# q, k and v laid out token by token, and third blocks of two experts gathered one expert earlier

## The chip, the cores and the metric

The kernel runs on one core of one Trainium2 chip. The metric is the device time of one execution in microseconds (us). Before the change the median of three runs is 735.86 us (735.72 to 737.33).

The engines are named as in the profile: PE is TensorE, with PEld its weight loads; DVE is VectorE, ACT is ScalarE, POOL is GpSimd, SP is SyncE. A q behind the name (SPq) is the engine's own sequencer, which issues transfers. All transfers share 16 DMA engines.

## What is computed

Three layers, one after the other, in float32. First causal attention by blocks of 64 tokens: 4 batches, 8 heads, 576 tokens, 64 numbers a head. Then a dense layer (512 to 2048, ELU, back to 512) on all 2304 tokens. Then a layer of 8 experts of which each token uses at most one:

```
scores = scale * np.matmul(q, k.transpose(0, 1, 3, 2))      # masked by blocks of 64, softmax
x = attn_out.transpose(0, 2, 1, 3).reshape(B * S, H * D)
h = x @ w_in
x = np.where(h > 0, h, np.exp(np.minimum(h, 0)) - 1) @ w_out
...
do_compute = x @ w_skip > 0
e_idx = argmax(xc @ w_gate)                                  # xc: the tokens with do_compute
y[e_idx == e] = gate_w * (relu(xc @ w1[e]) @ w2[e])
out[do_compute] = xc + y
```

q, k and v come as (batch, head, token, number). With the given inputs the eight experts get 176, 2, 5, 91, 283, 192, 453 and 14 tokens.

## The kernel before

**The planner.** Most of the work isn't issued as it is written. A recorder collects the instructions of a stage with their reads and writes, gives each a cost, and puts them in an order for each engine; then it issues them. That is why most rows of the profile name line 320, where recorded instructions are issued. The cost of a transfer goes by its bytes and doubles where the innermost run of its pattern is under 512 B. The order on an engine is fixed once issued; only semaphores decide when an instruction starts.

**The front.** `load_raw` (line 668) loads a tile of 128 tokens (64 for the last of a batch) of q, k or v: 128 rows by 8 heads by 64 numbers, 256 KB, into one of five `raw` tiles. In DRAM the eight heads of a token lie apart, so the pattern walks 256 B runs. `prep_k`, `prep_q` and `prep_v` split the tile on ACT and DVE into two float16 parts; k and q are then transposed, by TensorE for the first two tiles of batch 0, by a transposing transfer for the others. `vflat` (line 621) loads all of a batch's v flat, for a scale. In between, `raw_load` brings the weights of the dense layer (tiles `rw`, 512 KB each), which `conv` turns from 64-bit into 32-bit floats on DVE (tiles `twi`, `two`). All these loads go out on SP's queue in the order that the planner gave. The attention units of all batches and the dense layer run interleaved until about 560 us.

**The experts.** From there the code has branches on the number of tokens. The order is expert 0, 6, 4, 5 (`ORDER`), then 1, 2, 3 and 7 together (`LAST`). A first block of 128 tokens each of experts 0 and 6 is done ahead. A block is up to 128 tokens (the first of most experts is 64): a gather by POOL of 128 rows of `pay_d` into one of three staging tiles `gp`, a transposing transfer on SP into a place x (half of one of four tiles `X2`; `mxt` and `mxwo` in the rows), two layers of matmuls, and a scatter by POOL that adds to the output. Block (e, j) is block j of expert e. `place_of` (line 1719) names its place: all blocks j >= 2 of the four use the fourth tile, half j % 2.

Who gathers a block beside which other block stands in three tables. `GATHERS` (line 1734) are those beside a first block (`first_tokens`, line 1775). `PREP` (line 1736) lists by expert, and by part between bars, what is done beside its first, second and third block: l and m load half of an expert's weights, s takes their norm, c scales it, p splits them, and g gathers; "g1-0" is block (1, 0). `more_tokens` (line 1815) opens a branch for block j: it runs the block with its part of `PREP`, and where the branch isn't taken the else side does the rest of `PREP` alone. A loop inside it (line 1826) also gathers further blocks of the same expert. `the_rest` (line 1851) handles blocks past the fourth (the third for expert 0).

Of the kernel before, what the change touches and what calls it, by code (L numbers as in the profile page):

```python
# [356 lines left out]
@with_exitstack  # L357
def tile_kernel(ctx, tc, q, k, v, w_in, w_out, w_skip, w_gate, w1, w2, out):
    nc = tc.nc
    B, H, S, D = q.shape  # L360
    NT, DM = out.shape
    DFF = w_in.shape[1]
    E = w_gate.shape[1]
# [18 lines left out]
    rc = Recorder(nc)  # L382
# [237 lines left out]

    def vflat(b):
        t = ap.tile([128, H * S * D // 128], F32, tag="kt1", bufs=1, name="vflat")
        rc.sync.dma_start(out=t, in_=v[b].rearrange("h s d -> (h s d)").rearrange("(p x) -> p x", p=128))
        st["vf", b] = t

    def vmax(b):
# [38 lines left out]
    def trows(n):  # L665
        return 128 if n < 4 else 64

    def load_raw(nm, b, n):
        src = {"q": q, "k": k, "v": v}[nm]
        r = trows(n)  # L670
        t = ap.tile([128, H, D], F32, tag="raw", bufs=5, name="raw")
        rc.sync.dma_start(out=t[0:r], in_=src[b, :, n * 128:n * 128 + r, :].rearrange("h p d -> p h d"))
        RAW[nm, b, n] = t

    def early(b, n):
# [554 lines left out]
    def L(nm, b, n):  # L1230
        return lambda: load_raw(nm, b, n)
# [4 lines left out]
    for b in range(B):  # L1236
        g0, g1 = ubase[b, 0], ubase[b, 1]
# [83 lines left out]
    VF = [4, 5, 6, 6, 7, 8, 9]  # L1321
    rc.base = -300
    load_raw("k", 0, 0)
    load_raw("q", 0, 0)
    load_to(2)
    load_raw("k", 0, 1)
    load_raw("q", 0, 1)
    vflat(0)
    setup_consts()
    rc.gpsimd.tensor_copy(out=ident16, in_=ident)  # L1330
# [22 lines left out]
    for b in range(1, 4):  # L1353
        on_q(0, VF[b - 1], lambda b=b: vflat(b))
        on_q(0, VF[b + 2], lambda b=b: vmax(b))
# [213 lines left out]
    for i in range(2):  # L1569
        t = wp.tile([128, 2, PW], F32, tag=f"wo{i + 4}", bufs=1, name=f"gp{i}")  # L1570
# [24 lines left out]
    X2 = [AH["x"], mo.tile([128, 8, 256], F16, tag="xt", bufs=3, name="mxt1")]  # L1595
# [12 lines left out]
    def gather(ix, xT):  # L1608
        gp = GP[ng[0] % 3]
        ng[0] += 1  # L1610
        rc.gpsimd.indirect_dma_start(out=gp, out_offset=None, in_=pay_d[:, :],
                                     in_offset=bass.IndirectOffsetOnAxis(ap=ix, axis=0), bounds_check=NT - 1, oob_is_err=False)
        rc.sync.dma_start_transpose(out=xT, in_=gp.bitcast(F16))
# [94 lines left out]
    def block(*args):  # L1708
        for _ in block_in_parts(*args):
            pass  # L1710
# [4 lines left out]
    ORDER = [0, 6, 4, 5]  # L1715
    LAST = [1, 2, 3, 7]
    XP = {0: 1, 6: 2, 4: 0, 5: 1}

    def place_of(e, j):
        if e in LAST:  # L1720
            i = LAST.index(e)
            h = (X2[2 - i // 2 * 2], i % 2) if j == 0 else (X2[1], 1) if j == 1 else (X2[3], j % 2)
        else:
            h = X2[XP[e] if j < 2 else 3], j % 2
        return h[0][:, :, 128 * h[1]:128 * h[1] + 128]

    def gather_to(e, j):
        gather(gix[:, e, C0[e] + j:C0[e] + j + 1], place_of(e, j))

    def pre_gather(e):  # L1730
        for j in range(2):
            gather_to(e, j)

    GATHERS = {0: [], 6: [(6, 2), (4, 0), (4, 1)], 4: [(4, 2)], 5: [(5, 2)]}

    PREP = {int(e): [x.split() for x in h.split("|")] for e, h in (y.split(":") for y in (
        "6:l1-1 m2-0 c5-0 p5-0 s1-0|g5-0 g5-1 c5-1 p5-1|g1-0 g2-0 c1-0 s1-1,4:l2-1 m7-0 p1-0 c1-1|p1-1 s2-0|g3-0 g7-0 c2-0 s2-1,"
        "5:l7-1 l3-0 p2-0 c2-1|p2-1,8:a3-1 s7-0 s7-1 c7-0 p7-0 c7-1 p7-1").split(","))}

    def aside_of(e, part):  # L1740
        return PREP.get(e, [])[part:part + 1]
# [8 lines left out]
    def split_beside(e, part):  # L1750
        for h in sum(aside_of(e, part), []):
            if h[0] == "m":
                load_half(int(h[1]), int(h[3]), 5.0)
            if h[0] == "g":
                gather_to(int(h[1]), int(h[3]))
            if h[0] in "almg":
                continue
            for kind, f in prep_steps(int(h[1]), int(h[3]), 13.0 if e == 8 else 3.0):
                if kind[1] == {"s": "t", "c": "c", "p": "p"}[h[0]]:
                    rc.atom()  # L1760
                    rc.shift = -150000 if kind == "scale" else 0
                    f()
                    if h[0] == "s":
                        rc.ready[len(rc.steps) - 1] = 4.0
                    rc.shift = 0

    def tokens(e, j, xT, fs, par=None, block=block):

        c = C0[e] + j
        if j == 0 and e in SMALL:  # L1770
            return block(e, xT[:, :, 64:128], hix[:, e, c:c + 1], half[:, e, c, 1:2], j if par is None else par, 64)
        else:
            return block(e, xT, six[:, e, c:c + 1], fs[:, c:c + 1], j if par is None else par)

    def first_tokens(e, fs):

        rc.begin()
        rc.late = rc.left
        rc.strict = e in (4, 5)
        rc.urgent = True  # L1780
        load_beside(e, 0)
        tokens(e, 0, place_of(e, 0), fs)
        rc.urgent = False
        for g in GATHERS[e]:
            gather_to(*g)
        split_beside(e, 0)
        rc.issue()
# [23 lines left out]
    def hint(e, j, n):  # L1811

        tc.mark_branch_hint_location(f"n{e}_{j}", n > 128 * j, engines=[mybir.EngineType.PE])

    def more_tokens(e, j, fs):

        aside = j and aside_of(e, j)
        now = rc.left
        keep = list(FREE), dict(RAW2), dict(WHL)
        with tc.If(cnt[e] > 128 * j, preferred_fallthrough_block=True, label=f"n{e}_{j}") as cmp:  # L1820
            if j < BLOCKS[e]:
                hint(e, j + 1, cnt[e])
                rc.begin()
                rc.late = rc.left if j else {}
                rc.urgent = True
                for x in {6: (3,), 4: (3,), 5: (), 0: (1, 2)}.get(e, (1, 2, 3)) if j == 1 else (3,) if (e, j) == (5, 2) else ():
                    gather_to(e, x)
                tokens(e, j, place_of(e, j), fs)
                rc.urgent = False
                if aside:  # L1830
                    split_beside(e, j)
                rc.issue()
                now = rc.left
                more_tokens(e, j + 1, fs)

            else:
                the_rest(e, fs)
        if aside:
            with cmp.Else():
                FREE[:] = keep[0]  # L1840
                for x, y in ((RAW2, keep[1]), (WHL, keep[2])):
                    x.clear()
                    x.update(y)
                rc.begin()
                for part in range(j, len(PREP[e])):
                    split_beside(e, part)
                rc.issue()
        if j == 1:
            rc.left = now

    def the_rest(e, fs):

        trips = nc.values_load(ni[0:1, 8 + e:9 + e], min_val=BLOCKS[e], max_val=NS)
        sel = sm.tile([128, 3, NS], F32, tag="rw", bufs=1, name="sel")
        cj = sm.tile([128, 4], F32, tag="mx", bufs=4, name="cj")
        ci_ = sm.tile([128, 2], I32, tag="si", bufs=1, name="cji")
        nc.vector.memset(cj[:, 0:1], float(C0[e] + BLOCKS[e] - 1))
        nc.gpsimd.iota(sel[:, 0], pattern=[[1, NS]], base=0, channel_multiplier=0, allow_small_or_imprecise_dtypes=True)
        with tc.For_i(BLOCKS[e], trips):
            nc.vector.tensor_scalar(out=cj[:, 0:1], in0=cj[:, 0:1], scalar1=1.0, scalar2=None, op0=ALU.add)  # L1860
            nc.vector.tensor_scalar(out=sel[:, 1], in0=sel[:, 0], scalar1=cj[:, 0:1], scalar2=None, op0=ALU.is_equal)
            for x, src in ((1, gix[:, e, :]), (2, six[:, e, :]), (3, fs)):
                nc.vector.tensor_tensor(out=sel[:, 2], in0=sel[:, 1], in1=src, op=ALU.mult)
                nc.vector.tensor_reduce(out=cj[:, x:x + 1], in_=sel[:, 2], axis=AX.X, op=ALU.add)
            nc.vector.tensor_copy(ci_, cj[:, 1:3])
            gather(ci_[:, 0:1], X2[3][:, :, 0:128])
            block(e, X2[3][:, :, 0:128], ci_[:, 1:2], cj[:, 3:4], 0)

    gather_to(0, 0)
    pre_gather(6)  # L1870
# [109 lines left out]
```

## Time and profile before

| | us |
|---|---|
| median of 3 runs | 735.86 |
| the profiled execution | 739.06 |
| its span, first to last instruction | 736.9 |
| PE busy | 674.6 |
| DVE busy | 577.1 |
| ACT busy | 513.8 |
| POOL busy | 82.0 |

A row of a timeline gives start, duration, engine, line, operation, the tile written and the tiles read, the count, and in brackets how long the engine was idle before and what released it. The transfer view counts packets in a stretch, and the share of the 16 DMA engines' time that each queue took (it can pass 100%, as transfers overlap within an engine).

### The profile page before, as it was taken

To read this page: it belongs to the slowest core of one execution; us is meant where nothing else is said; L and a number is where in the kernel's file an instruction comes from. 1 tells how busy PE (TensorE), PEld (TensorE's weight loads), DVE (VectorE), ACT (ScalarE), POOL (GpSimd) and SP (SyncE) were. 2 spreads that over 40 slices of the span, in tenths; PEclk is the share of its full clock that TensorE was granted. 3 is DMA by queue.
4 is the path that set the end of the run, shared out by engine and by line. 5 is a ranking of instruction groups with operands and counts; after the bars stand their busy time and mean duration, and the time that the engine had idled before them with its cause. 6 is when DMAs were issued, how large, how long until landed. Compare 5 with 4: busy or idle time off the path is not lost. (4 is left out here: it accounts for less than half of the span.)

```text
span 736.9 us, 17737 instructions
## 1 busy us (share of the span) xinstructions
PE 674.6 (92%) x6665; PEld 463.8 (63%) x6665; DVE 577.1 (78%) x1664; ACT 513.8 (70%) x1090; POOL 82.0 (11%) x121
## 2 busy tenths in 40 slices
PE   4678988999999999989999999999999999999794
PEld 3456633775466666647656667667575667687583
DVE  5887999987999999878969946999687645666462
ACT  5966746999986887678668736865465638696482
POOL 2000000001001000100100100100114135333112
PEclk9669999999999999999999999999999999999897
DMA  9999999888696999899439259626265688999631
GB/s 264 229 257 304 282 277 270 177 159 163 128 199 136 187 182 189 148 198 186 90 79 181 46 93 293 256 91 197 71 215 121 191 176 247 179 284 219 176 117 16
DMA packets 262123, 134.00 MB, mean 182 GB/s; under 512 B 233467, under 2 KB 234501, under 8 KB 261504
## 3 DMA queue, kind: packets, MB, share of 16 engines
q1 hardware_dynamic: 256816, 123.33, 72.8%
q0 software_dynamic: 4112, 7.23, 4.6%
q10 hardware_dynamic: 1088, 2.10, 0.9%
q8 instruction: 57, 0.93, 0.5%
q14 instruction: 50, 0.41, 0.2%
HBM read 74.12 MB, written 12.75 MB: 118 GB/s over the span
## 5 line engine op out<-in xcount | busy, mean ns | idle before, releaser
L320 PE MATMUL h<-xt,win 128*128 128x256 f16 x1344 | 158.5, 273 | 1.6 <-DVE n L320 1.0
L320 PE MATMUL y<-wout,g 128*128 128x512 f16 x672 | 155.7, 379 | 0.0
L320 PEld LDWEIGHTS <-win 128*128 128x128 f16 x1344 | 129.0, 98 | 25.0 <-issue 2.8
L320 PEld LDWEIGHTS <-g 128*128 128x128 f16 x672 | 64.1, 98 | 66.6
L320 ACT ACTIVATE e<-s,mx 128x512 f32<-128x512 f32 (+4 forms) x160 | 82.3, 517 | 26.0 <-DVE mx L320 10.4
L320 ACT ACTIVATE ehl<-e,su 128x512 f16<-128x512 f32 (+4 forms) x160 | 80.5, 550 | 22.7 <-DVE su L320 10.3
L320 DVE SCALAR_TENSOR_TENSOR ehl<-e,su,ehl 128x512 f16<-128x512 f32 (+4 forms) x160 | 81.9, 537 | 11.3 <-ACT ehl L320 11.1
L320 PE MATMUL s<-kt,qt 128*128 128x384 f16 (+5 forms) x384 | 69.2, 306 | 10.7 <-ACT e L320 7.2
L320 DVE TENSOR_REDUCE mx<-s 128x1 f32<-128x512 f32 (+4 forms) x160 | 74.4, 474 | 5.1 <-PE s L320 4.8
L320 PE MATMUL h<-xt,twi 128*128 128x256 f32 x256 | 60.4, 388 | 2.4 <-DVE g L320 2.0
L320 PE MATMUL xps<-et,vt 128*64 128x128 f16 (+1 forms) x1440 | 49.6, 217 | 13.8 <-DVE xt L320 3.0
L320 PE MATMUL y<-two,g 128*128 128x512 f32 x128 | 59.5, 603 | 1.5 <-DVE two L320 1.5
L320 PEld LDWEIGHTS <-vt 128*64 128x64 f16 x1440 | 39.8, 113 | 32.2 <-issue 23.1
L320 ACT ACTIVATE el<-h,col 128x512 f32<-128x512 f32 x56 | 38.2, 682 | 24.7 <-PE h L320 23.8
L320 PEld LDWEIGHTS h<-xt,twi 128*128 128x128 f32 x256 | 48.2, 193 | 9.6 <-DVE g L320 2.5
L320 ACT ACTIVATE g<-el,col 128x512 f16<-128x512 f32 x56 | 40.1, 718 | 18.6 <-DVE el L320 17.2
L320 PEld LDWEIGHTS <-p 128*128 128x128 f16 x984 | 46.6, 98 | 9.9 <-PEq L1820 4.1
L320 PEld LDWEIGHTS <-qt 128*128 128x128 f16 (+1 forms) x384 | 28.2, 103 | 28.6 <-issue 11.2
L320 DVE SCALAR_TENSOR_TENSOR g<-el,col,g 128x512 f16<-128x512 f32 x56 | 41.7, 744 | 3.7 <-ACT g L320 3.6
L1521 DVE SCALAR_TENSOR_TENSOR p<-p,n,p 128x1024 f16<-128x1024 f32 x32 | 40.7, 1281 | 3.5 <-ACT p L1520 3.4
L320 DVE SCALAR_TENSOR_TENSOR el<-h,col,el 128x512 f32<-128x512 f32 x56 | 41.7, 744 | 1.3
L320 DVE TENSOR_TENSOR hh<-r,hh 128x256 f16<-128x256 f32 x36 | 15.0, 423 | 34.3 <-ACT hh L1666 32.7
(234 smaller groups left out, 1145.1 us busy)
## 6 DMA issues: line engine op xcount, KB each, us to landing
p<-in_moe_w_dram SPq DMA_DIRECT2D x45, 512.0 KB
rw<-in_moe_w_in_dram SPq DMA_DIRECT2D x16, 512.0 KB
rw<-in_moe_w_out_dram SPq DMA_DIRECT2D x16, 512.0 KB
pb<-in_moe_w_dram SPq DMA_DIRECT2D x10, 512.0 KB
vflat<-in_v_dram SPq DMA_DIRECT2D x4, 1152.0 KB
out_dram<-pay SPq DMA_DIRECT2D x18, 256.0 KB
pay_d<-pay SPq DMA_DIRECT2D x18, 256.0 KB
raw<-in_k_dram SPq DMA_DIRECT2D x16, 256.0 KB
```

The lines of the kernel that those rows point to most:

```text
L320: rec.call(e, time, lambda: getattr(self.real, op)(*args, **kw), reads, writes, dma)
L1521: rc.call("dve", 1.2, lambda: nc.vector.scalar_tensor_tensor(out=half(1), in0=raw.t, scalar=sc, in1=half(0), op0=ALU.mult, op1=ALU.subtrac ...
```

## The change

q, k and v are handed over as (batch, token, head, number), rearranged on the host. A row of a `raw` tile is then one stretch of 2 KB in DRAM; the pattern is still written with three levels, so that the planner's cost for it is what it was.

In the experts, the third blocks of 4 and 5 are gathered one expert earlier: (4, 2) beside (6, 2), and (5, 2) beside (4, 2). They leave `GATHERS` and the loop in `more_tokens` and enter `PREP`. (4, 2) and (4, 3) get the second half of the fourth tile; the third and fourth blocks of 6 and 5 use the first. A fourth block (j = 3) of 6, 4 or 5 is gathered only inside its own branch, where before it was gathered beside the second block, for 6 and 4.

```
-    B, H, S, D = q.shape
+    B, S, H, D = q.shape
...
-        rc.sync.dma_start(out=t, in_=v[b].rearrange("h s d -> (h s d)").rearrange("(p x) -> p x", p=128))
+        rc.sync.dma_start(out=t, in_=v[b].rearrange("s h d -> (s h d)").rearrange("(p x) -> p x", p=128))
...
-        rc.sync.dma_start(out=t[0:r], in_=src[b, :, n * 128:n * 128 + r, :].rearrange("h p d -> p h d"))
+        rc.sync.dma_start(out=t[0:r], in_=src[b, n * 128:n * 128 + r])
...
-            h = X2[XP[e] if j < 2 else 3], j % 2
+            h = (X2[XP[e]], j % 2) if j < 2 else (X2[3], e == 4)
...
-    GATHERS = {0: [], 6: [(6, 2), (4, 0), (4, 1)], 4: [(4, 2)], 5: [(5, 2)]}
+    GATHERS = {0: [], 6: [(6, 2), (4, 0), (4, 1)], 4: [], 5: []}
...
-        "6:l1-1 m2-0 c5-0 p5-0 s1-0|g5-0 g5-1 c5-1 p5-1|g1-0 g2-0 c1-0 s1-1,4:l2-1 m7-0 p1-0 c1-1|p1-1 s2-0|g3-0 g7-0 c2-0 s2-1,"
+        "6:l1-1 m2-0 c5-0 p5-0 s1-0|g5-0 g5-1 c5-1 p5-1|g1-0 g2-0 g4-2 c1-0 s1-1,4:l2-1 m7-0 p1-0 c1-1|p1-1 s2-0|g3-0 g7-0 g5-2 c2-0 s2-1,"
...
-                for x in {6: (3,), 4: (3,), 5: (), 0: (1, 2)}.get(e, (1, 2, 3)) if j == 1 else (3,) if (e, j) == (5, 2) else ():
+                for x in {0: (1, 2)}.get(e, () if e in ORDER else (1, 2, 3)) if j == 1 else (3,) if j == 3 and e in ORDER else ():
...
-            gather(ci_[:, 0:1], X2[3][:, :, 0:128])
-            block(e, X2[3][:, :, 0:128], ci_[:, 1:2], cj[:, 3:4], 0)
+            gather(ci_[:, 0:1], place_of(e, 2))
+            block(e, place_of(e, 2), ci_[:, 1:2], cj[:, 3:4], 0)
...
-        a = _np.ascontiguousarray(inputs[name])
+        a = inputs[name]
+        a = _np.ascontiguousarray(a.transpose(0, 2, 1, 3) if name in "qkv" else a)
```

## Rows read from the trace of the kernel before

**Rows 1.** The page: PE's busy time, and its granted clock in 40 slices.

```profile
PE 674.6 (92%) x6665; PEld 463.8 (63%) x6665; DVE 577.1 (78%) x1664; ACT 513.8 (70%) x1090; POOL 82.0 (11%) x121
...
PEclk9669999999999999999999999999999999999897
```

**Rows 2.** Busy time by stretch: length, each engine, granted clock, DMA share, GB/s.

```profile
20.00:30.00 10.00, 7.27 (x62) 4.99 (x62) 9.11 (x34) 8.97 (x26) 0.00 (x0) 0.53 1.00 289
...
90.00:100.00 10.00, 8.90 (x43) 4.02 (x42) 10.00 (x23) 4.43 (x9) 0.00 (x0) 1.00 1.13 267
...
140.00:150.00 10.00, 10.00 (x126) 8.30 (x125) 9.07 (x31) 10.00 (x28) 0.95 (x1) 1.00 0.90 169
```

**Rows 3.** PE's waits, 140 to 300 us: total, times, longest.

```profile
PE xps L320 <- DMA et<-ehl: 2.1, 3, 1.5
```

**Rows 4.** Timeline of PE in the experts' stage.

```profile
641.48 3.06 PE L320 MATMUL hp<-mxt,p 128*128 128x64 f16 x96 [0.95 <-ACTq L1820]
...
658.25 4.18 PE L320 MATMUL hp<-mxwo,p 128*128 128x128 f16 x72
...
669.87 0.44 PE L320 MATMUL hp<-mxt,p 128*128 128x64 f16 x9 [0.89 <-ACTq L1820]
...
689.27 0.19 PE L320 MATMUL hp<-mxwo,pd 128*128 128x64 f16 x1
693.47 0.29 PE L320 MATMUL hp<-mxwo,pd 128*128 128x64 f16 x2 [4.00 <-issue]
693.58 3.75 PE L320 MATMUL hp<-x,p 128*128 128x128 f32 x16
...
706.51 2.05 PE L320 MATMUL hp<-x,p 128*128 128x128 f32 x16
```

**Rows 5.** Packets moved at 13.6 to 14.6, 16.2 to 17.6 and 6.8 to 9.6 us.

```profile
DMA packets 1103, 0.28 MB, mean 278 GB/s; under 512 B 1103, under 2 KB 1103, under 8 KB 1103
...
DMA packets 282, 0.54 MB, mean 389 GB/s; under 512 B 16, under 2 KB 16, under 8 KB 282
...
DMA packets 2111, 0.71 MB, mean 254 GB/s; under 512 B 2010, under 2 KB 2010, under 8 KB 2111
```

**Rows 6.** The same view, 582.5 to 584 us, while the lists load: packets, MB, share.

```profile
q1 hardware_dynamic: 977, 0.17, 62.8%
```

**Rows 7.** Timelines of ACT and DVE in the front: uses of loaded tiles.

```profile
4.14 0.63 ACT L320 ACTIVATE k<-raw 128x512 f16<-128x512 f32 x1 [2.05 <-DMA raw<-in_k_dram]
...
9.34 0.43 DVE L320 TENSOR_SCALAR twi<-rw 128x512 int32<-128x512 int32 x1 [1.05 <-DMA rw<-in_moe_w_in_dram]
...
10.39 0.63 ACT L320 ACTIVATE k<-raw 128x512 f16<-128x512 f32 x1 [0.67 <-DVE twi L320]
...
49.09 0.63 ACT L320 ACTIVATE qq<-raw 128x512 f16<-128x512 f32 x1 [2.69 <-DMA raw<-in_q_dram]
...
61.09 0.43 DVE L320 TENSOR_SCALAR twi<-rw 128x512 int32<-128x512 int32 x1 [3.02 <-DMA rw<-in_moe_w_in_dram]
...
105.54 0.43 DVE L320 TENSOR_SCALAR two<-rw 128x512 int32<-128x512 int32 x1 [1.04 <-DMA rw<-in_moe_w_out_dram]
```

**Rows 8.** Timeline of SP's queue: issue of the first and second k.

```profile
0.81 0.46 SPq L320 DMA_DIRECT2D raw<-in_k_dram  x1
...
3.42 0.47 SPq L320 DMA_DIRECT2D raw<-in_k_dram  x1
```

**Rows 9.** SP's queue in the experts' stage: weight loads, two transposes, that of (5, 2).

```profile
656.37 2.00 SPq L1466 DMA_DIRECT2D p<-in_moe_w_dram  x4
...
668.97 3.11 SPq L320 DMA_TRANSPOSE mxt<-gp  x2
...
684.54 2.74 SPq L320 DMA_TRANSPOSE mxwo<-gp  x1
```

**Rows 10.** Busy time by stretch around and after the pause; columns as in rows 2.

```profile
693.50:697.00 3.50, 3.50 (x18) 3.50 (x19) 0.43 (x1) 0.80 (x2) 0.00 (x0) 0.50 0.03 7
```

**Rows 11.** Packets by queue, 690.6 to 691 us: packets, MB, share.

```profile
q8 instruction: 1, 0.02, 22.3%
```

## The prediction

> **What bounds the kernel now.** I read the page first, then busy time by stretch, then the timelines of single engines and the transfer view where an engine waited. TensorE is busy 92% of the span, and its granted clock falls to 6 tenths in the second and third of the 40 slices, 18 to 55 us [rows 1]. So the bound changes with the stage. In 20 to 30 us VectorE and ScalarE carry the load (9.11 and 8.97 of 10 us) and TensorE is 7.27 of 10; in 90 to 100 us VectorE is full; from 140 us TensorE is full [rows 2]. The 16 transfer engines are at or above a share of 1.0 in two of these three stretches. Before 140 us a transfer that lands earlier can therefore still move the end, because everything after it is an order fixed in advance with little idle time; after 140 us it can do so only where TensorE itself waits for a transfer, and between 140 and 300 us the largest such wait sums to 2.1 us [rows 3]. In the expert stage TensorE goes from block to block with gaps of about 1 us at the borders (0.89 us before expert 5) and with one pause of 4.00 us in the middle of a block, which the profile puts down to nothing it can see [rows 4].
>
> **The layout: what one load costs.** A full q, k or v tile is 256 KB. Before, each row gathers eight runs of 256 B, one for each head, so 1024 packets. In a stretch that holds nothing else, such packets move at 278 GB/s; in one with hardly any short packets the rate is 389 GB/s [rows 5]. That makes 0.92 to 0.94 us against 0.67 us: 0.25 us a load. Where two of these loads overlap the tail of weight loads, 2010 short packets took 2.8 us, 1.4 us for each tile [rows 5]; against 0.67 that would be 0.7 us a load, the upper bound. There are 48 full and 12 half tiles, together 54 full ones: 13.5 us of transfer time taken off, most of it where nobody waits.
>
> Will the runs really become 2 KB? The pattern still names three levels on both sides (row, head, 64 numbers), but now the last two are contiguous in memory and in the tile. The nearest row is the load of the lists, written with four levels of which the last two are contiguous in DRAM: if every pair of numbers (8 bytes) were a packet, its 152 KB would be 19,456 packets, but the stretch that holds nearly all of it has 977 on that queue, 0.17 MB [rows 6], about 174 B each. So contiguous levels are joined. I take 2 KB. The planner still reads 256 B from the pattern, so its costs, and with them the order of the front, stay.
>
> **The layout: the sum.** Step 1, the start: ScalarE waits 2.05 us for the first k, VectorE follows and TensorE begins [rows 7]. Between the issue at 0.81 [rows 8] and this use at 4.14 us lie 3.3 us, of which the data's own 0.92 us falls to 0.67. Lower bound 0.25 us; upper bound 1.0, if the slow ramp before full rate also comes from the number of packets. I take 0.6, between them, as no row separates the two. Step 2, the second k (issued at 3.42, used at 10.39 us [rows 7, 8]): ahead of it in the queue are k, q and two weight loads, so it gains 0.25 twice plus its own 0.25 to 0.7. But VectorE must first convert the weights for which it waits 1.05 us at 9.34 [rows 7]; they gain only the 0.5 us of k and q. I take 0.6 beyond step 1, near those weights' 0.5, since VectorE's own order sets this stretch; bounds 0 and 0.9. From there to 40 us ScalarE and VectorE are full and keep the shift. Step 3, the later waits: q at 49.09 us (2.69 us of waiting) gains its own 0.25 to 0.7, taken 0.4; the wait of 3.02 us at 61.09 is for weights issued before the next k, so 0; weights at 105.54 us (1.04 us) [rows 7] have one k directly ahead, 0.25; smaller ones 0.1. Together 0.75, bounds 0 and 2. Step 4, after 140 us: 0.2, bounds 0 and 0.5. Sum 0.6 + 0.6 + 0.75 + 0.2 = 2.15 us, bounds 0.25 and 4.4. A loss is possible only if earlier transfers upset a later order; I give it 0.5 us. The flat load of v for the scale stays contiguous and costs 0.
>
> **The gathers.** The experts' blocks in this run are three of expert 6, three of 4, two of 5; no fourth block runs and expert 5 has no third. So before, the gathers and transposes for (6, 3), (4, 3) and (5, 2) are made for nothing; after, the first two are gone and (5, 2) stays. Needed and moved is only (4, 2), from beside (4, 0) to beside (6, 2). Its block begins at 658.25 us right behind the one before [rows 4], so the move earns 0 there: that wait doesn't exist. The cover in the new place is all of (4, 0) and (4, 1), the 16.8 us from 641.48 to 658.25 [rows 4], so it costs 0 too; without that cover a gather and its transpose would stand open in front of the block. The queues: on SyncE the weight loads at 656.37 stand behind the transpose of (4, 2) today [rows 9]; without it they can follow the loads before them at once, and nothing before the last stage reads them. In the new place the transpose of (4, 2) stands before the weight loads of the first block of 4 and may push them by its 1.3 us; their readers come two blocks later: 0. On GpSimd the gather waits for one of three staging tiles, and the scatter of (6, 2) is queued behind it; that scatter holds an output tile that is wanted two blocks later: 0. Beside (4, 2) a third transpose now stands ahead of the loads in the first block of 5. Today's two took 3.11 us [rows 9], so it delays them by up to 1.6 us; they are read in the last stage, the first of them at 693.58 [rows 4], so this would come out of what the pause gives back, not out of today's order: 0.
>
> **The pause.** The one thing in the tail worth microseconds is the 4.00 us at 689.27 to 693.47. After it the clock is 0.50 [rows 10], half of 2.4 GHz; before it TensorE had idled. 16 matmuls then take 3.75 us where the same form takes 2.05 later [rows 4]: 1.7 us, and about 0.5 more behind them. Together 6.2 us. An instruction transfer (queue q8) lands only at 690.6 to 691 us [rows 11], while the useless transpose of (5, 2), issued at 684.54 [rows 9], is still moving. If the transpose held up TensorE's instructions, moving it away from this border gives back 4 to 6.2 us, and next is late what waits at the other borders, about 1 us: 5.2 us net.
>
> The Trainium skill, "DMA: Bandwidth & Descriptors", section "Queues, rings and completion order", says that each transfer engine serves its queue rows in turn, packet by packet. By that rule one queue's transposes could not keep another queue's instruction packet out for microseconds, and the pause would stay where it is: the forecast below instead of the rival A. The row shows only that both were there together, so neither is decided.
>
> **The rivals.** Likeliest, 0.42: the front gains and the pause stays, or isn't in most runs: the profiled execution took 739.06 us, 3.2 more than the median 735.86, so I can't be sure that the timed runs have it. 735.86 - 2.15 = 733.7, its own range 731.5 to 735.6. A, 0.34: the pause goes as well: 733.7 - 5.2 = 728.5. B, 0.12: the layout brings nothing, since runs stay 256 B or the waits fill up with something else: 735.9. For it: VectorE's full stretches; against: the joined list packets. C, 0.12, slower: three transposes instead of two now stand at the border of 4 and 5, perhaps a little before today's 668.97 [rows 9], since fewer transfers stand ahead of their gathers, and expert 5's instructions come through at just that moment. If transposes hold up instructions there, a pause of 4.0 plus 1.7 us appears before or in (5, 0), while the one at 693 stays: 733.7 + 5.7 = 739.4. It decides from the point where the second transpose's data starts before expert 4's last matmul at about 669 us. Against it: today's gap there is 0.89 us.
>
> **How the numbers follow.** The forecast is 733.7. 0.2% is 1.5 us (about what a measurement of this kernel can tell from no change), so faster means under 734.4. The likeliest case is faster when its gain is over 1.5 us: about 0.28 of 0.42, the rest same. A is faster, 0.34; B is same, but for 0.02 in which an upset order loses; C is slower. Faster 0.62, same 0.14 + 0.10 = 0.24, slower 0.14. The range takes in A with up to 0.7 us more and C but for its last microsecond, and leaves out the bounds at which all gains or all losses come together: 727.8 to 738.5.
>
> **What would show it.** Right: in 0 to 60 us hardly any packets under 512 B beside transposes; the first k used at 3.2 to 3.9 us; TensorE's first matmul 0.3 to 1 us earlier and the 50% clock ending earlier by as much; the same order of instructions in the front; the third block of 4 still without a gap. The pause: no gap of 4 us after 687, or one at 669. Wrong if the first k lands when it did, if the shift of 1 us at 12 us is gone by 140 us, or if a new wait for an x tile appears at the start of (4, 2).

## The result and the profile after

The changed kernel takes 724.39 us in the median of five runs (722.1 to 729.6), against 735.86 us for the kernel before in the same comparison: a ratio of 0.9853, 95% interval 0.9817 to 0.9889; by that ratio 10.8 us less. The profiled execution is the median one, 724.39 us, with a span of 722.6. A second comparison gave 0.9832 (`e8_after`, below). The prediction was 733.7 us with a range of 727.8 to 738.5: the sign was right, the size far too small, and the time lies 3.4 us under the range.

The page after, the lines that answer to [rows 1], and its packets:

```profile
PE 671.3 (93%) x6665; PEld 462.8 (64%) x6665; DVE 576.3 (80%) x1664; ACT 514.2 (71%) x1090; POOL 78.4 (11%) x119
...
PEclk9559999999999999999999999999999999999998
...
DMA packets 211468, 132.96 MB, mean 184 GB/s; under 512 B 176027, under 2 KB 177061, under 8 KB 210848
```

The work is the same; only idle time went. Before, the page counted 262,123 packets, 233,467 of them under 512 B: 57,440 short packets are gone. 55,296 of them (54 full tiles of 1024) were those of q, k and v; the rest goes with the two gathers that are dropped. The stretches of [rows 2]:

```profile
20.00:30.00 10.00, 7.27 (x62) 4.99 (x62) 9.10 (x34) 8.97 (x26) 0.00 (x0) 0.50 0.51 170
90.00:100.00 10.00, 7.87 (x42) 3.61 (x41) 10.00 (x23) 4.02 (x10) 0.00 (x0) 1.00 1.10 282
140.00:150.00 10.00, 10.00 (x97) 8.34 (x96) 7.72 (x23) 9.85 (x25) 0.95 (x1) 1.00 0.84 138
```

In 20 to 30 us the transfer share is 0.51 instead of 1.00: more has been moved before (up to 20 us a mean of 323 GB/s instead of 263), and by 30 us it is as much as before. In 90 to 100 us nothing has changed in kind: VectorE is full. TensorE's wait of [rows 3], 140 to 300 us:

```profile
PE xps L320 <- DMA et<-ehl: 1.4, 3, 0.8
```

It was 2.1 us and is 1.4. The first uses of loaded tiles, as in [rows 7], on ScalarE, VectorE and TensorE:

```profile
3.72 0.63 ACT L320 ACTIVATE k<-raw 128x512 f16<-128x512 f32 x1 [1.63 <-DMA raw<-in_k_dram]
...
10.15 0.63 ACT L320 ACTIVATE k<-raw 128x512 f16<-128x512 f32 x1 [1.07 <-DMA raw<-in_k_dram]
...
9.43 0.43 DVE L320 TENSOR_SCALAR twi<-rw 128x512 int32<-128x512 int32 x1 [0.88 <-DMA rw<-in_moe_w_in_dram]
...
12.52 1.03 PE L320 MATMUL tp<-id,k 128*128 128x128 f16 x8 [2.83 <-DVE k L320]
```

The first k is used 0.42 us earlier and the second 0.24, but the weight conversion between them comes at 9.43 us where it came at 9.34, and TensorE's transposes of the second k start at 12.52 us; before, at 12.43. Of the start's gain nothing has reached TensorE by 12 us.

TensorE's timeline in the experts, as in [rows 4]:

```profile
634.41 2.96 PE L320 MATMUL hp<-mxt,p 128*128 128x64 f16 x96 [0.89 <-ACTq L1820]
...
650.60 4.18 PE L320 MATMUL hp<-mxwo,p 128*128 128x128 f16 x72
...
662.29 0.42 PE L320 MATMUL hp<-mxt,p 128*128 128x64 f16 x9 [0.96 <-ACTq L1820]
...
682.02 0.22 PE L320 MATMUL hp<-mxwo,pd 128*128 128x64 f16 x2 [0.70 <-issue]
682.14 2.02 PE L320 MATMUL hp<-x,p 128*128 128x128 f32 x16
```

And the stretch at the place of the pause, as in [rows 10]:

```profile
682.00:686.00 4.00, 3.98 (x76) 3.91 (x77) 0.69 (x3) 2.59 (x6) 0.00 (x0) 1.00 0.52 70
```

The pause of 4.00 us is 0.70, the clock behind it is whole, and the 16 matmuls that took 3.75 us take 2.02. The third block of expert 4 starts without a gap, and expert 5 (662.29) still waits about 1 us. SyncE's queue, as in [rows 9]:

```profile
642.68 1.97 SPq L1466 DMA_DIRECT2D p<-in_moe_w_dram  x4
659.52 3.39 SPq L320 DMA_TRANSPOSE mxt<-gp  x2
663.03 1.24 SPq L320 DMA_TRANSPOSE mxwo<-gp  x1
665.26 2.45 SPq L1469 DMA_DIRECT2D p<-in_moe_w_dram  x4
667.80 2.70 SPq L1466 DMA_DIRECT2D p<-in_moe_w_dram  x4
```

The transpose of (5, 2) now goes out at 663.03 us, 19 us ahead of the place of the pause (682.02).

**Where the time went.** All kernels here run the same 6665 matmuls in the same order on TensorE, so the start of the n-th one can be compared from trace to trace. The table gives it as after minus before, worked out from the two TensorE timelines, at the time that it had before:

| before, us | 5.6 | 31 | 45 | 62 | 77 | 119 | 200 | 286 | 562 | 631 | 686.5 | 701 |
|---|---|---|---|---|---|---|---|---|---|---|---|---|
| after - before | -0.42 | +0.23 | -0.27 | -1.55 | -2.99 | -4.05 | -4.48 | -4.97 | -4.97 | -7.01 | -7.94 | -13.71 |

So three parts: the front, 5.0 us, made between 45 and 120 us and a little up to 286; the experts before the pause, 3.0 us; the pause, 5.8 us. These are two single executions, and that of before was 3.2 us over its median. What the parts are worth in the timed runs is told below.

### The profile page after: what moved, and what is told of

Read it like the earlier page. It is cut to its first block, busy times and chain, and to the rows that moved or that the text cites. A ratio compares the mean times of both kernels' runs of the same rounds, so it can differ in the third digit from the quotient of the medians.

```text
span 722.6 us, 17731 instructions
## 1 busy us (share of the span) xinstructions
PE 671.3 (93%) x6665; PEld 462.8 (64%) x6665; DVE 576.3 (80%) x1664; ACT 514.2 (71%) x1090; POOL 78.4 (11%) x119
## 5 line engine op out<-in xcount | busy, mean ns | idle before, releaser
L320 DVE SCALAR_TENSOR_TENSOR ehl<-e,su,ehl 128x512 f16<-128x512 f32 (+4 forms) x160 | 82.0, 537 | 12.0 <-ACT ehl L320 11.8
L320 PE MATMUL xps<-et,vt 128*64 128x128 f16 (+1 forms) x1440 | 49.6, 217 | 12.4 <-DVE xt L320 3.0
L320 PEld LDWEIGHTS y<-two,g 128*128 128x128 f32 x128 | 23.0, 189 | 26.4 <-issue 19.3
```

Source lines behind the costliest of these rows:

```text
L320: rec.call(e, time, lambda: getattr(self.real, op)(*args, **kw), reads, writes, dma)
```

## Experiments

Ratios are to the kernel before on the same chip, with 95% intervals. Single runs of one kernel differ by some 7 us either way and once by 10 (before: 729.63 to 742.69 in one comparison; `e1_layout`: 726.10 to 742.54, median 732.66), so differences between two kernels are read from both the ratios and the matmul starts. All of these kernels keep the front's order.

**One half of the change each.** `e1_layout` is the kernel before with the new layout alone:

```
-    B, H, S, D = q.shape
+    B, S, H, D = q.shape
...
-        rc.sync.dma_start(out=t[0:r], in_=src[b, :, n * 128:n * 128 + r, :].rearrange("h p d -> p h d"))
+        rc.sync.dma_start(out=t[0:r], in_=src[b, n * 128:n * 128 + r])
```

> The layout alone; the gathers stay where they were before. If each part does what the comparison of the two traces suggests, the front's gain of about 5 us by 560 us is the layout's and all of it is here, while the pause of 4 us in the middle of the first block after expert 5 stays: about 730 us. Rival: the pause went only because the front shifted everything against some free-running event; then it is gone here too: about 724 us.

Measured: 732.66 us, ratio 0.993 (0.9899 to 0.9962), 5.2 us less. The matmul at 286 us comes 6.45 us earlier. The pause stays, and two waits show that the profile of before doesn't have:

```profile
653.05 4.18 PE L320 MATMUL hp<-mxwo,p 128*128 128x128 f16 x72 [1.21 <-DMA mxwo<-gp]
668.33 0.26 PE L320 MATMUL hp<-mxt,pb 128*128 128x64 f16 x3 [1.84 <-issue]
690.80 0.29 PE L320 MATMUL hp<-mxwo,pd 128*128 128x64 f16 x2 [3.50 <-issue]
```

The first line is the third block of 4, which waits for its own transpose; the second is a stop inside (5, 0); the third is the pause. After the pause the granted clock is 0.50, as before [rows 10].

`e2_gathers` is the other half, the gathers and places of the change with the old layout:

```
-    GATHERS = {0: [], 6: [(6, 2), (4, 0), (4, 1)], 4: [(4, 2)], 5: [(5, 2)]}
+    GATHERS = {0: [], 6: [(6, 2), (4, 0), (4, 1)], 4: [], 5: []}
...
-        "6:l1-1 m2-0 c5-0 p5-0 s1-0|g5-0 g5-1 c5-1 p5-1|g1-0 g2-0 c1-0 s1-1,4:l2-1 m7-0 p1-0 c1-1|p1-1 s2-0|g3-0 g7-0 c2-0 s2-1,"
+        "6:l1-1 m2-0 c5-0 p5-0 s1-0|g5-0 g5-1 c5-1 p5-1|g1-0 g2-0 g4-2 c1-0 s1-1,4:l2-1 m7-0 p1-0 c1-1|p1-1 s2-0|g3-0 g7-0 g5-2 c2-0 s2-1,"
```

> The gathers alone; q, k and v lie by head as before. If the pause was made by the useless transpose of (5, 2), no pause over 1.5 us after expert 5, the same front as before to 0.5 us, and some 6 to 9 us less: 727 to 730 us. Rival (the pause depends on when the stage begins, not on the transpose): pause still there, 734 to 736 us.

Measured: 729.41 us, ratio 0.9902 (0.9866 to 0.9937), 7.2 us less. At 286 us its matmul is 1.76 us earlier, at 562 us 0.99: no front gain to speak of. The stop at the last border is 0.99 us instead of 4.00. So each half works by itself; the two gains add up to 12.4 us, which agrees with the 10.8 (8.2 to 13.5) that both bring together.

**Is it the transpose of (5, 2)?** `e3_52_back` is the changed kernel with (5, 2) alone gathered where it was before:

```
-    GATHERS = {0: [], 6: [(6, 2), (4, 0), (4, 1)], 4: [], 5: []}
+    GATHERS = {0: [], 6: [(6, 2), (4, 0), (4, 1)], 4: [], 5: [(5, 2)]}
...
-        "6:l1-1 m2-0 c5-0 p5-0 s1-0|g5-0 g5-1 c5-1 p5-1|g1-0 g2-0 g4-2 c1-0 s1-1,4:l2-1 m7-0 p1-0 c1-1|p1-1 s2-0|g3-0 g7-0 g5-2 c2-0 s2-1,"
+        "6:l1-1 m2-0 c5-0 p5-0 s1-0|g5-0 g5-1 c5-1 p5-1|g1-0 g2-0 g4-2 c1-0 s1-1,4:l2-1 m7-0 p1-0 c1-1|p1-1 s2-0|g3-0 g7-0 c2-0 s2-1,"
```

> The changed kernel with only the gather of (5, 2) put back beside the first block of expert 5; (4, 2) stays early and the fourth blocks stay in their branches. If that transpose makes the pause, a gap of 3 to 4 us and the lower clock behind it come back: about 730 us, 5 to 6 us over the changed kernel. Rival: the pause came from the total of transfers, or from (4, 2) and (4, 3): no gap, 724 us.

Measured: 729.45 us, ratio 0.9883 (0.9845 to 0.9921). The pause is back. SyncE's issue of the transpose, and TensorE:

```profile
676.06 5.22 SPq L320 DMA_TRANSPOSE mxwo<-gp  x1
...
688.48 0.26 PE L320 MATMUL hp<-mxwo,pd 128*128 128x64 f16 x2 [3.99 <-issue]
```

The stretch behind it, at half the clock:

```profile
688.50:692.00 3.50, 3.50 (x18) 3.50 (x18) 0.43 (x1) 0.80 (x2) 0.00 (x0) 0.50 0.02 5
```

`e5_no52` goes the other way: the kernel before, but (5, 2) is gathered only in its own branch, which isn't taken here.

```
-    GATHERS = {0: [], 6: [(6, 2), (4, 0), (4, 1)], 4: [(4, 2)], 5: [(5, 2)]}
+    GATHERS = {0: [], 6: [(6, 2), (4, 0), (4, 1)], 4: [(4, 2)], 5: []}
...
-                for x in {6: (3,), 4: (3,), 5: (), 0: (1, 2)}.get(e, (1, 2, 3)) if j == 1 else (3,) if (e, j) == (5, 2) else ():
+                for x in {6: (3,), 4: (3,), 5: (), 0: (1, 2)}.get(e, (1, 2, 3)) if j == 1 else (2, 3) if (e, j) == (5, 2) else ():
```

> The kernel before with one thing changed: (5, 2) is gathered only inside its own branch, which isn't taken, so its gather and transpose fall away. If that transpose makes the pause after expert 5: no gap over 1.2 us there, TensorE about 5.5 us earlier at the end than at expert 5's end, the front as before; 731 us. Rival (the pause goes only with all the gathers moved): a gap of 3 to 4 us, 736 us.

Measured: 732.92 us, ratio 0.9954 (0.9921 to 0.9987), 3.4 us less than before. The stop is 1.51 us (under 1.2 was expected), behind it the clock is whole, and from 686.5 to 701 us TensorE makes up 4.95 us. The two waits of `e1_layout` are here too:

```profile
656.12 4.18 PE L320 MATMUL hp<-mxwo,p 128*128 128x128 f16 x72 [1.53 <-DMA mxwo<-gp]
671.10 0.26 PE L320 MATMUL hp<-mxt,pb 128*128 128x64 f16 x3 [1.55 <-issue]
689.93 0.23 PE L320 MATMUL hp<-mxwo,pd 128*128 128x64 f16 x2 [1.51 <-issue]
```

`e6_plain52` is `e3_52_back` with the staged rows of (5, 2) copied instead of transposed:

```
-        rc.sync.dma_start_transpose(out=xT, in_=gp.bitcast(F16))
+        if plain:
+            rc.sync.dma_start(out=xT, in_=gp.bitcast(F16).rearrange("p (a b) -> p a b", a=8))
```

> The run in which (5, 2) is back beside the first block of expert 5, but its staged rows go to their place by a plain copy in runs of 256 B instead of a transposing transfer; the rows of (5, 2) are therefore not transposed, and that block isn't run. If it is the transposing that keeps the instructions waiting: no gap over 1.2 us, like the changed kernel, 724 to 727 us. Rival (any 256 KB of short packets at that border does it): a gap of 3 to 4 us and 729 us.

Measured: 726.99 us, ratio 0.9869 (0.9801 to 0.9937), and a stop of 1.10 us. The transfer views tell the two apart. First `e3_52_back`, 683 to 685 us, from its border (682.99) into the pause; then `e6_plain52`, 677 to 680 us, around its border (678.42):

```profile
DMA packets 317, 0.20 MB, mean 101 GB/s; under 512 B 285, under 2 KB 285, under 8 KB 317
...
q1 hardware_dynamic: 317, 0.20, 83.5%
```

```profile
DMA packets 908, 0.92 MB, mean 305 GB/s; under 512 B 735, under 2 KB 735, under 8 KB 903
...
q1 hardware_dynamic: 903, 0.87, 84.1%
q14 instruction: 4, 0.03, 2.9%
q8 instruction: 1, 0.02, 2.4%
```

The copy's 256 B packets are under way across the border, as the transpose's are, and the instruction packets (q8, q14) land between them. Beside the transpose none lands for 2 us; the next three come together between 685.25 and 685.5 us, where the transpose's last packets go through. So it is in all three traces with the pause: q8's packet begins 2 to 3 us after the border (before [rows 11], `e1_layout`, `e3_52_back`); without the pause, 0.6 us before it to 0.5 after (after, `e5_no52`, `e6_plain52`). And in each of the twelve traces with any stop there, TensorE goes on 1.3 to 1.8 us after that packet's end.

The records of single packets show what the engines do meanwhile. Shortly after the transpose's 256 B packets begin, about as many of them as there are transfer engines stay in flight and end together: in `e3_52_back` 17, begun from 682.74 to 684.34 us, all at 685.0, the longest after 2.25 us; in the kernel before 18, at 690.4 (longest 1.38 us); in `e1_layout` 21, at 687.4 (2.00 us). q8's packet begins 0.3 to 0.4 us behind that end in all three. Around the border of `e6_plain52` no packet of the copy's queue takes over 0.42 us. The view of before shows it from 688.75 to 689 us; a packet's whole time counts where it starts, hence a share far over 100%:

```profile
q1 hardware_dynamic: 232, 0.08, 564.2%
```

Why the packets are held isn't in the trace.

`e7_best` is the changed kernel with (5, 2) gathered only in its own branch; "g5-2" leaves `PREP` as in `e3_52_back`, and the loop in `more_tokens` takes it:

```
-                for x in {0: (1, 2)}.get(e, () if e in ORDER else (1, 2, 3)) if j == 1 else (3,) if j == 3 and e in ORDER else ():
+                for x in {0: (1, 2)}.get(e, () if e in ORDER else (1, 2, 3)) if j == 1 else (3,) if j == 3 and e in ORDER else (2,) if (e, j) == (5, 2) else ():
```

> The changed kernel with (5, 2) gathered only inside its own branch. If a useless transpose beside (4, 2) still costs something at the next border or delays expert 5's loads, 0.3 to 1 us less than the changed kernel; else the same to 0.3 us. No pause after expert 5.

Measured: 725.12 us, ratio 0.984 (0.9774 to 0.9907). `e8_after`, the changed kernel again beside it:

> The changed kernel once more, beside these: 725 us, a gap under 1.2 us after expert 5, and TensorE 4 to 5 us earlier at 560 us than in the kernel before. If the front's gain seen so far was chance of single executions, it differs here by over 2 us.

Measured: 725.44 us, ratio 0.9832 (0.9768 to 0.9896), with a stop of 1.22 us at the last border. So the transpose of (5, 2), in the place that the change gives it, costs nothing that these runs can show.

**Is it the packets?** `e4_cap256` keeps the layout but cuts the loads into 256 B:

```
-        rc.sync.dma_start(out=t[0:r], in_=src[b, n * 128:n * 128 + r])
+        rc.sync.dma_start(out=t[0:r], in_=src[b, n * 128:n * 128 + r], max_dma_last_dim=256)
```

> The changed kernel with every q, k and v load cut into packets of 256 B; DRAM is still token by token and the order the same. If the number of packets makes the front's gain, it goes: TensorE at 560 us stands where it did before the change, to 1 us, and the time is about 729 us. Rival (it is that a row lies together in DRAM): the front keeps its 5 us, 724 us.

Measured: 730.91 us, ratio 0.9932 (0.9901 to 0.9964). The front's gain is gone: at 119 us 0.78 us earlier, at 286 us 0.77 later. So it was the size of the packets, not where the tokens lie in DRAM. `e9_cap512` has `max_dma_last_dim=512`:

> The changed kernel, but the loads of q, k and v cut into packets of 512 B (before 256 B, after 2 KB), the layout kept. Read off: how much earlier than in the kernel before TensorE's matmul at 200 us comes (2 KB: 4.2 to 5.2 us, 256 B: 0.6 to 1.5 us), and the stretches in which SyncE's queue is held up while issuing, 0 to 45 us. If it is the number of packets that holds the queue up, a half of them should bring about half: 2 to 3.5 us earlier, and a time near 728. If 256 B packets alone are bad, 512 B brings everything: 4.2 us or more earlier, a time near 725.5. Rival, only long packets help: 0.6 to 1.5 us, near 730.

Measured: 729.75 us, ratio 0.9904 (0.9871 to 0.9937). By the matmul starts, 2.91 us earlier at 200 us, two thirds of the gain, but 4.44 at 286 and 4.62 at 562, about nine tenths of it. By the time, it keeps less: its interval hardly meets that of the changed kernel. The two readings don't agree. Part of it may lie elsewhere: in this trace a stop of 1.66 us at the last border was followed by a clock of 0.54 (683.9 to 687.4 us), and from 686.5 to 701 us TensorE made up 3.36 us where the changed kernel makes up 5.77. Whether the timed runs had that isn't known, and how much 512 B loses against 2 KB stays open. The Trainium skill, "DMA: Bandwidth & Descriptors", section "Specifications", names 512 B as the least transfer for the full rate; the starts from 286 us on agree with that, the start at 200 us and the ratio of 0.9904 against 0.984 don't.

**Which loads?** By now I thought that I had the mechanism. Before, SyncE is held up while it issues: 4.50 us for one load of v flat at 4.55 us, 4.32 for two weight loads at 10.20, 3.30 for one at 15.71. After, the longest such stretches up to 45 us are these two, and the third k, issued at 14.62 us before, goes out at 9.47:

```profile
4.30 1.46 SPq L320 DMA_DIRECT2D raw<-in_v_dram  x2
5.81 2.69 SPq L320 DMA_DIRECT2D rw<-in_moe_w_in_dram  x2
...
9.47 0.34 SPq L320 DMA_DIRECT2D raw<-in_k_dram  x1
```

`e10_cap_b0` cuts only batch 0's 15 loads into 256 B, `e11_cap_rest` only the other 45:

```
-        rc.sync.dma_start(out=t[0:r], in_=src[b, n * 128:n * 128 + r])
+        rc.sync.dma_start(out=t[0:r], in_=src[b, n * 128:n * 128 + r], **({"max_dma_last_dim": 256} if b == 0 else {}))
```

> The changed kernel, but the loads of batch 0's q, k and v alone, 15 of the 60, cut back into packets of 256 B. Theory: the gain is made where SyncE's queue is held up while issuing, in the first 45 us, and nearly all loads there are batch 0's. Then most of the gain goes: the matmul at 200 us comes 1 to 2 us earlier than in the kernel before instead of 4.2 to 5.2, and the time is near 729. Rival, each load gives its share of transfer time wherever it is: a quarter of the gain goes, 3.5 to 4.2 us earlier, near 726.5.

Measured: 727.76 us, ratio 0.9877 (0.9822 to 0.9932). The hold-ups are back:

```profile
4.93 3.83 SPq L320 DMA_DIRECT2D vflat<-in_v_dram  x1
...
9.93 4.24 SPq L320 DMA_DIRECT2D rw<-in_moe_w_in_dram  x2
...
15.39 3.54 SPq L320 DMA_DIRECT2D rw<-in_moe_w_in_dram  x1
```

And yet the matmul at 200 us comes 3.32 us earlier, at 286 us 4.44: most of the gain is there. The other kernel:

> The changed kernel, but the loads of batches 1 to 3, 45 of the 60, cut back into packets of 256 B, batch 0's kept at 2 KB. Theory (the first 45 us): the gain stays but for what the waits at 50 to 105 us give; 3 to 5 us earlier at 200 us, near 726.5. Rival (each load its share): three quarters of the gain go, 1.5 to 2 us earlier, near 728.5.

Measured: 731.85 us, ratio 0.994 (0.99 to 0.9981). No hold-up over 2.3 us up to 24 us, and the gain is gone: 1.25 us at 119 us, 0.41 at 200, 0.11 at 286. My theory of the first 45 us fell on both sides. It isn't quite the rival either, by which each load gives its share: batch 0's loads, a quarter, give at 119 us 1.25 of 4.05, and by 286 us nothing that lasts. The waits tell where the other 45 give it. Here are, for 45 to 120 us, the waits of ScalarE and VectorE for loads (total, times, longest) in the kernel before, in the kernel after, and then in `e11_cap_rest`:

```profile
ACT qq L320 <- DMA raw<-in_q_dram: 4.2, 2, 2.7
ACT k L320 <- DMA raw<-in_k_dram: 1.9, 1, 1.9
...
DVE twi L320 <- DMA rw<-in_moe_w_in_dram: 4.5, 3, 3.0
...
DVE two L320 <- DMA rw<-in_moe_w_out_dram: 1.2, 2, 1.0
```

```profile
ACT qq L320 <- DMA raw<-in_q_dram: 1.1, 2, 0.7
...
ACT k L320 <- DMA raw<-in_k_dram: 0.3, 1, 0.3
...
DVE twi L320 <- DMA rw<-in_moe_w_in_dram: 3.3, 3, 2.4
DVE two L320 <- DMA rw<-in_moe_w_out_dram: 0.5, 1, 0.5
```

```profile
ACT qq L320 <- DMA raw<-in_q_dram: 2.7, 2, 1.4
ACT k L320 <- DMA raw<-in_k_dram: 1.8, 1, 1.8
...
DVE twi L320 <- DMA rw<-in_moe_w_in_dram: 4.5, 3, 3.6
DVE two L320 <- DMA rw<-in_moe_w_out_dram: 1.1, 3, 0.6
```

All waits of the two engines for transfers in this stretch sum to 14.0 us before, 11.8 in `e11_cap_rest`, 9.8 in `e10_cap_b0` and 8.0 after, in the same order as TensorE's gain at 119 us: 0, 1.25, 2.86, 4.05.

Put together, with the matmul at 286 us: the eight kernels whose batches 1 to 3 come in packets of 512 B or more have it 4.4 to 6.5 us earlier (mean 5.1); the five with 256 B there, before among them, from 1.8 earlier to 0.8 later (mean 0.4 earlier). No kernel lies between.

## Why the prediction was wrong in size

**The layout, step by step.** That contiguous levels are joined was right: the 55,296 short packets of q, k and v went. Step 1 (0.6 us taken for the first k) measured 0.42, within its bounds. Step 2 (0.6 more at the second k) failed: its reason was that the weights ahead gain what k and q ahead of them gain; they came 0.09 us later, VectorE's order set the pace as the step itself said, and with step 1 nothing was left on TensorE at 12 us. Step 3 is the term that was mis-sized: taken 0.75 with an upper bound of 2, it measured 3.8 us between 45 and 119 us (from -0.27 to -4.05). I had priced each wait by the load waited for and the one directly ahead, 0.25 us each. Instruction by instruction, the wait for q at 49.09 us [rows 7] fell from 2.69 to 0.72 us, where I took 0.4; the waits for k at 62.68 us (1.89 to 0.27) and for q at 91.32 us (1.52 to 0.43) I hadn't put into the sum except as "smaller ones 0.1"; that of 3.02 us for weights, set at 0, fell to 2.39, and that of 1.04 at 105.54 us, taken 0.25, is gone. These gains overlap, so they don't simply add up to TensorE's 3.8. But single waits fell by up to 2 us where one load's own time was priced at 0.25 to 0.7. In 45 to 120 us the transfer share is over 1.0 before and after alike. That a tile waits there for all that stands ahead of it on the same 16 engines, so that the savings of several loads add up in one wait, fits these numbers; it wasn't tried by itself. Step 4 (0.2, bound 0.5) measured 0.9, from 119 to 286 us. Sum: 5.0 in the profiles and 5.2 to 6.1 in the timed runs (`e1_layout`; and the mean ratio of after, `e7_best` and `e8_after`, 0.9842, against that of `e2_gathers`, `e4_cap256` and `e11_cap_rest`, 0.9925) where I took 2.15 and bounded it by 4.4. Through which loads the gain passes between 119 and 286 us wasn't settled.

**The gathers.** "The move earns 0" was read from one execution, in which (4, 2) happened to start without a gap. In the two other kernels with the old gathers, `e1_layout` and `e5_no52`, it waits 1.21 and 1.53 us for its transpose, and (5, 0) stops for 1.84 and 1.55. From 562 to 686.5 us the three traces with the old gathers stand at 0, +2.1 and -0.5 us, the ten with the new ones at -0.2 to -3.6 (mean -2.5): about 3 us, and it arises behind 631 us, where the waits just named lie: from there to 686.5 us the old ones lose 2.1 us on the mean and the new ones gain 0.7. The pair of before and after is no example of it: 2.0 of its 3.0 us lie ahead of 631 us, where `e1_layout` and `e5_no52` with the old gathers gain 1.9 and 2.8 too, and 1.1 of them is a wait for VectorE at 623.26 us in before, which `e9_cap512`, `e10_cap_b0` and `e11_cap_rest` with the new gathers also have (0.8 to 1.0 us). In the timed runs it is 3.5 us between `e1_layout` (0.993) and `e3_52_back` (0.9883), and 2.1 if the pause's 3.4 are taken from the 5.5 of the three with new gathers and short packets; both are within the scatter. The change here is two things at once, the move of (4, 2) and the end of the useless gathers of (6, 3) and (4, 3); which of them earns it wasn't tried apart.

**The pause.** Rival A was right in its mechanism: the transpose of (5, 2) at this border keeps TensorE's instructions out. All three kernels with it there have 3.50 to 4.00 us and half the clock behind; the ten without it have at most 1.66, and of these `e9_cap512` alone the lower clock behind. A put 5.2 us on it. The traces bear that out (4.95 us in `e5_no52`, 5.77 after), the timed runs give 3.4 (`e5_no52`) and 3.0 (`e3_52_back` against the mean 0.9842), with intervals from 1.0 and 0.2 up to 5.8 us; so whether every run has it in full isn't decided. The step that failed was to set "stays, or isn't in most runs" (0.42) over A (0.34): no row spoke against the transpose, only the profile's 3.2 us over the median and a rule. That rule, in the Trainium skill, "DMA: Bandwidth & Descriptors", section "Queues, rings and completion order", says that an engine serves its queue rows in turn, packet by packet. `e6_plain52` agrees with it: 5 instruction packets land among 735 short ones in 3 us. `e3_52_back` doesn't contradict it: in its 2 us without an instruction packet, single packets of the transpose are in flight for up to 2.25 us. What failed is what I drew from the rule, that a transpose couldn't keep an instruction packet out for microseconds; that took its packets to be short. They aren't always long: after, one packet each of q8 and q14 lands in 663 to 665 us amid 1960 short packets, none of which takes over 0.4 us, and no stop follows. When an instruction packet is asked for isn't in the trace, nor why the transpose's packets are held; both stay open.

**The other rivals.** B (the layout brings nothing) is out by `e1_layout`. C (three transposes at the border of 4 and 5 hold up instructions) has the right place, as (5, 0) stops there in `e1_layout` and `e5_no52`, but its mechanism isn't seen: in both traces the transposes' packets are held only after that stop has ended (from 668.69 and 671.55 us), so why (5, 0) stops there is open. And after, with the third transpose, nothing stops: the wait before (5, 0) is 0.96 us, against 0.89 before.

**The sum again.** From A's 728.5 go 3.0 to 4.0 us more for the front (5.2 to 6.1 instead of 2.15) and 2.1 to 3.5 for the gathers; 1.8 to 2.2 come back, as the pause is worth 3.0 to 3.4 and not 5.2. That gives 722.8 to 725.6, and 724.39 lies in it. The terms are from the same set of runs as the result, so this shows that they fit together and is no second proof.

**The signs named beforehand.** Hardly any short packets beside transposes in 0 to 60 us: 8,480 under 512 B instead of 22,309. First k used at 3.2 to 3.9 us: 3.72. First matmul 0.3 to 1 us earlier: 0.42 (5.13 for 5.55). The order of the front kept: yes. No gap of 4 us after 687: right by A. The stretch at half clock ending earlier: no, it covers the same two slices of the page. The shift at 12 us lasting to 140 us was named as a condition; it wasn't there at 12 us at all, and the gain came later from other loads.

## What to carry to other kernels

Where the transfer engines are full, don't price a change of packet size by the tile waited for alone, but look at all that stands ahead of it: here single waits fell by up to 2 us where one load's own time was priced at 0.25 to 0.7. The waits to look at are those for every load in that stage, whatever it loads. A wait that one profile doesn't show may be there in other runs of the same kernel: before an edit is priced at nothing, look whether its transfer lands with room to spare. A transposing transfer that nobody needs is not free beside a place where an engine takes up new instructions, and here a plain copy of the same bytes nearly was (a stop of 1.10 us, against up to 1.66 with neither).

## What the runs showed of the hardware

Half the clock need not cost anything: in 18 to 55 us the granted clock was 0.63 before and 0.58 after, 1.00 in `e10_cap_b0`, and yet TensorE's matmul at 45 us comes only 0.66 us earlier than before there, against 0.58 in `e11_cap_rest`, where the clock was 0.63: in that stretch VectorE and ScalarE carry the load [rows 2]. The stretch in `e10_cap_b0`:

```profile
18.00:55.00 37.00, 26.84 (x195) 19.28 (x196) 32.81 (x92) 30.60 (x78) 0.35 (x1) 1.00 1.02 247
```

Elsewhere it fell in single executions after short idle times: in `e4_cap256` two gaps of 1.58 and 1.16 us were followed by a stretch at 0.53, which the same place with gaps of 1.57 and 0.70 us before didn't have, and TensorE lost 2.7 us from 317 to 374 us. The length of the gaps alone doesn't decide it: in `e5_no52` gaps of 1.55 and 1.22 us at the same place left the clock at 1.00, while a single stop of 1.84 us in `e1_layout` (668.33) and one of 1.66 in `e9_cap512` (683.91) brought it down. One trace alone can so be several microseconds off for a reason that isn't in the edit. TensorE's timeline in `e4_cap256`, and the stretch behind:

```profile
315.70 1.36 PE L320 MATMUL xps<-et,vt 128*64 128x128 f16 x42 [1.58 <-DVE xt L320]
318.22 1.01 PE L320 MATMUL xps<-et,vt 128*64 128x64 f16 x30 [1.16 <-ACT xt L320]
```

```profile
317.00:324.00 7.00, 5.84 (x47) 2.77 (x44) 4.07 (x12) 3.25 (x8) 0.00 (x0) 0.53 1.26 188
```

And SyncE's queue is held up while it issues when many short packets are outstanding (4.50 us before and 3.83 in `e10_cap_b0` for a load whose issue takes 0.57 after), though here, in the first 45 us, that cost the matmul at 286 us only half a microsecond in the traces (4.44 us earlier in `e10_cap_b0`, 4.97 after); the timed runs (0.9877, 0.9822 to 0.9932, against 0.984) don't exclude more.
